# Reordering loads, transposes, a mask and V casts in the opening stage of a fused attention and feed-forward kernel

## The chip, the cores and the metric

The kernel runs on one core of a Trainium2 chip. The metric is the device time of one execution in microseconds (us), lower is better. "Faster" and "slower" are at 2%. Single executions of one kernel here scatter (the kernel before 309.19 to 310.24 us), so every comparison rests on several runs of each kernel on the same chip.

## The reference, cut to what matters

Eight batches of eight heads, 576 positions, head dimension 64, in float32. Attention is causal within a window of 64 positions; its output is then taken through a gated feed-forward layer.

```
scores = scale * q @ k.T;   mask = (rel >= 0) & (rel < 64)
attn   = softmax(where(mask, scores, -1e9))
x      = (attn @ v) as [4608, 512]
h      = x @ w_in                      # w_in  [512, 2048]
g      = h * clip(h + 3, 0, 6) / 6
out    = g @ w_out                     # w_out [2048, 512]
```

## The kernel before

The kernel treats one batch after the other and interleaves two streams on TensorE. While the feed-forward layer of batch b runs ("pieces" of it are released by `run(m, n)` or `go(n)`), the attention of batch b+1 is prepared: Q and K are loaded in float32, cast to bf16 by GpSimd, turned by TensorE (transposes against an identity), copied from PSUM by VectorE or ScalarE, then scores, exponential, mask, product with V. Weights of the feed-forward layer arrive during the same time.

All edits lie in the opening: the first feed-forward stage (batch 0) with the attention of batch 1 beside it, roughly 17 to 56 us of the span. A 576-row sequence is 4 blocks of 128 rows and 64 leftover rows; the "rest" is those leftover rows. `w_out` comes in four parts of 512 KB. Loads issued by GpSimd share one queue, those of SP (the sync engine) another: POOLq and SPq in the profiles.

```
    ld.main(0, 4, 8)                       # Q of heads 4-7 of batch 1, by GpSimd
    ld.main(1, 4, 8)                       # K of heads 4-7
    ...
    bt.cast_qk(st, 0, 0, 4, pcopy)         # pcopy is a GpSimd copy, acopy a ScalarE one
    w_out += [load_w_out(4 * i, 4 * i + 4) for i in (1, 2)]
    bt.cast_rest_runs(rst1, pcopy)
    bt.cast_qk(st, 1, 0, 4, pcopy)
    vst1, end = load_v_end(1)
    after(end, w_out[0], "weights go first")
    rst0, _ = load_rest_runs(0, "rst0")    # rest of Q and K of batch 0, by SP
    rvst0 = load_v_rest_of_first()         # rest of V of batch 0, 128 KB, by SP
    cast_pairs(bt, st, 4, 4)               # casts Q and K of heads 4-7
    w_out.append(load_w_out(12, 16))
    insv = load_v(1, vst1, 0, H, nc.gpsimd)   # V of batch 1, one load for a head
    ...
    bt.main_t(0, 1, h_tr())()
    RR(bt, st_tr(1))                       # rest transposes of batch 1, one bank
    run(m)
    bt.main_t(1, 1, next(st_tr(0)))()      # K transposes of a pair, the other bank
    bt.cast_v_end(vst1, pcopy)
    for h in range(0, H, 2):
        bt.cast_v(vst1, h, h + 2, pcopy)   # two GpSimd casts each
    st2, ins2 = load_for_dma(2, (0,))      # Q of batch 2, by SP
    after(ins2[0], insv[2], "the values go first")
    ...
    def S1_(g, u, bank):
        scores(bt, g, u, bank=bank)()
        if u:
            masked(bt, g)                  # 0.96 us of VectorE, the last one 1.41 us
    ...
    SS1_(3)
    go()
    RR(bt0, st_tr(0))                      # rest of batch 0: transposes, then two copies
    acopy(out=bt0.V[SR:P, KB - 1, :, 0:D], in_=rvst0[SR:P, :, :])
    go(2)
    rest_s(bt0, 1)                         # scores of the rest: reads the copied KT
```

`run` and `go` advance the feed-forward work; `tr`, `st` and `h` are PSUM tiles. The tile framework inserts semaphores from the tiles that instructions touch; the program order on each engine is the order of these statements.

The softmax here doesn't subtract the row's maximum and nothing guards it: scores larger than these inputs give would overflow.

## Time and profile before

| | before |
|---|---|
| median of the first 3 runs | 309.38 us (309.19 to 310.20) |
| median of 6 runs beside the changed kernel | 309.61 us (309.19 to 310.24) |
| span in the profiled execution | 308.9 us, from a run of 310.71 us |
| TensorE busy | 97% |
| next busiest | VectorE and ScalarE, 57% each |
| first feed-forward product of batch 0 starts | 17.63 us |
| from there to the first product of the next token block | 38.86 us |
| from there to the end of TensorE's work | 249.16 us |

The last three rows cut the span at two starts of the same source line. The first of them holds the attention of batch 0, which runs ahead of everything that the change edits. The traces record TensorE's full clock from 4.07 us on in before, and until then a 128x512 matmul takes 634 ns and starts 427 ns after the one before it, afterwards 379 and 216, so the rate starts at half. The second is the stage which the change edits. The third is a stretch in which TensorE is never idle. The profiled run was slower, so a span read from it must not be set against a timed median.

### The profile page before, as it was taken

The page shows a single profiled execution, that of the slowest core. Times are in us where ns is not written, and L with a number is a line of the kernel's source. Part 1 is how long each engine was busy: PE and PEld are TensorE (multiplying, and loading weights), DVE is VectorE, ACT ScalarE, POOL GpSimd, SP SyncE. Part 2 cuts the span into 40 slices and gives each one's busy share as a digit, 9 for nine tenths or more (in the row PEclk, how much of TensorE's full clock was granted, in tenths as well). Part 3 has the DMA queues.
Part 4 walks back from the last instruction along what each step waited for, and adds up shares of the span by engine and source line. Part 5 has one row for each costly group of instructions (what it writes and reads, how often), then busy time and mean ns, then how long its engine had stood idle before and what let it go on. Part 6 is the DMA issues. An engine that isn't in the chain of part 4 may idle for free.

```text
span 308.9 us, 5688 instructions
## 1 busy us (share of the span) xinstructions
PE 300.5 (97%) x2194; PEld 150.2 (49%) x2194; DVE 176.1 (57%) x331; ACT 176.4 (57%) x266; POOL 98.4 (32%) x137
## 2 busy tenths in 40 slices
PE   7899999999999999999999999999999999999995
PEld 3454444644654454445444554455445544444444
DVE  4559545585646882678357834784377537306700
ACT  3857745686737851794179516971588157317711
POOL 5874477634633460426041704071400000000000
PEclk9999999999999999999999999999999999999999
DMA  7999998999999995999999989999910630010011
GB/s 245 201 207 268 259 233 182 245 269 215 189 203 275 206 192 141 246 217 217 171 253 211 216 151 252 208 213 163 245 45 2 134 89 0 34 70 34 0 70 68
DMA packets 141771, 52.80 MB, mean 171 GB/s; under 512 B 128688, under 2 KB 136752, under 8 KB 141744
## 3 DMA queue, kind: packets, MB, share of 16 engines
q1 hardware_dynamic: 135808, 43.73, 71.2%
q0 software_dynamic: 5520, 8.39, 13.0%
q8 instruction: 17, 0.28, 0.4%
q10 hardware_dynamic: 416, 0.33, 0.3%
q14 instruction: 10, 0.08, 0.1%
HBM read 36.70 MB, written 9.44 MB: 149 GB/s over the span
## 4 chain that ended last, share of the span: by engine, by line
PE 85%; DMA 10%; POOL 2%; issue 1%; DVE 1%; SPq 1%; ACT 0%; POOLq 0%
PE o L646 19%; PE acc L646 17%; PE h L580 17%; PE acc L580 6%; PE st L580 6%; PE o L580 6%; DMA qst<-in_q_dram 5%; DMA wout<-in_moe_w_out_dram 4%; PE st L377 4%; PE h L407 2%; PE h L646 2%; PE h L412 1%; DMA vst<-in_v_dram 1%; POOL V L260 1%; POOL win L239 1%
## 5 line engine op out<-in xcount | busy, mean ns | idle before, releaser
L580 PEld LDWEIGHTS <-win 128*128 128x128 bf16 x576 | 54.9, 98 | 63.9 <-DMA win<-in_moe_w_in_dram 0.4
L646 PEld LDWEIGHTS <-gT 128*128 128x128 bf16 x560 | 51.3, 98 | 56.9 <-issue 0.8
L646 PE MATMUL o<-wout,gT 128*128 128x512 bf16 x272 | 66.0, 380 | 0.0
L580 PE MATMUL h<-xT,win 128*128 128x512 bf16 x260 | 62.7, 379 | 0.0
L646 PE MATMUL acc<-wout,gT 128*128 128x512 bf16 x256 | 60.0, 379 | 0.0
L385 ACT ACTIVATE pT<-st 128x768 bf16<-128x768 f32 x64 | 48.5, 808 | 16.6 <-PE st L377 16.5
L588 DVE SCALAR_TENSOR_TENSOR gT<-t,st 128x512 bf16<-128x512 bf16 (+1 forms) x26 | 19.5, 766 | 55.6 <-ACT t L587 55.5
L588 DVE SCALAR_TENSOR_TENSOR gT<-t,h 128x512 bf16<-128x512 bf16 x65 | 43.7, 684 | 11.0 <-ACT t L587 10.9
L587 ACT ACTIVATE t<-h,half 128x512 bf16<-128x512 f32 x65 | 43.9, 692 | 7.7 <-PE h L580 7.7
L395 DVE TENSOR_TENSOR pT<-pT,mask 128x1536 bf16<-128x1536 bf16 x28 | 29.6, 1057 | 23.5 <-ACT pT L385 23.4
L652 ACT COPY osb<-acc 128x512 f32<-128x512 f32 x16 | 9.4, 587 | 42.7 <-PE acc L646 42.7
L260 POOL CAST V<-vst 128x512 bf16<-128x512 f32 (+1 forms) x14 | 17.0, 1221 | 51.7 <-DMA vst<-in_v_dram 51.5
L270 POOL CAST qn<-qst 128x512 bf16<-128x512 f32 x24 | 17.9, 783 | 42.7 <-DMA qst<-in_q_dram 33.1
L580 PE MATMUL st<-xT,win 128*128 128x512 bf16 x120 | 28.9, 379 | 0.0
L652 ACT COPY osb<-o 128x512 f32<-128x512 f32 x17 | 10.0, 588 | 29.4 <-PE o L646 29.4
L580 PE MATMUL acc<-xT,win 128*128 128x512 bf16 x100 | 26.2, 379 | 0.0
L580 PE MATMUL o<-xT,win 128*128 128x512 bf16 x96 | 25.1, 379 | 0.0
L429 DVE TENSOR_TENSOR opg<-h,rec 128x320 bf16<-128x320 f32 x48 | 23.6, 491 | 1.9 <-DVE rec L426 0.3
L587 ACT ACTIVATE t<-st,half 128x512 bf16<-128x512 f32 (+1 forms) x26 | 19.3, 754 | 5.7 <-PE st L580 5.5
L407 PEld LDWEIGHTS <-pT 128*128 128x128 bf16 x256 | 17.4, 97 | 7.6 <-PE h L453 0.5
L587 ACT ACTIVATE t<-acc,half 128x512 bf16<-128x512 f32 x25 | 17.2, 688 | 4.7 <-PE acc L580 4.1
L588 DVE SCALAR_TENSOR_TENSOR gT<-t,acc 128x512 bf16<-128x512 bf16 x25 | 17.1, 684 | 3.5 <-ACT t L587 3.5
(115 smaller groups left out, 296.0 us busy)
## 6 DMA issues: line engine op xcount, KB each, us to landing
out_dram<-osb SPq DMA_DIRECT2D x31, 256.0 KB, 2.5
qst<-in_q_dram SPq DMA_DIRECT2D x28, 256.0 KB, 4.7
vst<-in_v_dram SPq DMA_DIRECT2D x24, 256.0 KB, 5.3
kst<-in_k_dram SPq DMA_DIRECT2D x23, 256.0 KB, 5.6
wout<-in_moe_w_out_dram POOLq DMA_DIRECT2D x4, 512.0 KB, 13.8
vst<-in_v_dram SPq DMA_DIRECT2D x15, 128.0 KB, 3.3
win<-in_moe_w_in_dram POOLq DMA_DIRECT2D x3, 512.0 KB, 8.7
qst<-in_q_dram POOLq DMA_DIRECT2D x2, 512.0 KB, 12.6
```

The costliest lines, as they stand in the source:

```text
L260: copy(out=self.V[:, 0 : KB - 1, h0:h1, 0:D], in_=vst[:, 0 : KB - 1, h0:h1, :])
L270: pcopy(out=n[:, g, 0 : KB - 1, :, :].rearrange("p k h d -> p k (h d)"), in_=s[:, 0 : KB - 1, 2 * g : 2 * g + 2, :].rearrange("p k h d -> ...
L377: nc.tensor.matmul(st[:, h, o0 : o0 + n], lhsT=bt.KT[h * D : (h + 1) * D, g, k0 : k0 + P], rhs=bt.QT[h * D : (h + 1) * D, g, q0 : q0 + n], ...
L385: nc.scalar.activation(out=pT[:, :, 2 * u : 2 * u + 2, 0:QW], in_=st[:, :, 0:w].rearrange("p h (k w) -> p h k w", k=2), func=EXP, scale=scale,
L395: nc.vector.tensor_tensor(out=pT[:, :, :, 0:QW], in0=pT[:, :, :, 0:QW], in1=mask[:].rearrange("p (h k) w -> p h k w", h=2), op=MULT,)
L407: nc.tensor.matmul(ob, lhsT=pT[:, h, qb, 0:P], rhs=V[:, qb, 2 * g + h, :], start=True, stop=(qb == 0),)
L429: nc.vector.tensor_tensor(out=opgs[bt.b, g][:, 0:nb, h, :], in0=ov[:, :, 0:D], in1=rec[:, 0:nb].unsqueeze(2).to_broadcast([P, nb, D]), op= ...
L580: nc.tensor.matmul(hT, lhsT=win16[:, g, fc * P : (fc + 1) * P], rhs=xT[:, g, t0 : t0 + TB], start=(g == 0), stop=(g == NG - 1),)
L587: nc.scalar.activation(out=t1[:], in_=hT, func=RELU, bias=half[:], scale=1.0 / 6.0)
L588: nc.vector.scalar_tensor_tensor(out=out, in0=t1[:], scalar=1.0, in1=hT, op0=MIN, op1=MULT,)
L646: nc.tensor.matmul(accs[ts], lhsT=gT[:, fc, ts * P : (ts + 1) * P], rhs=wout16[:, fc, :], start=(fc == 0), stop=(fc == NFC - 1),)
L652: acopy(out=osb[:], in_=accs[ts])
```

## The change

The intent: bring the second part of `w_out` earlier, so that TensorE does not wait for it; take waits out of the rest transposes; lighten GpSimd by casting V in larger pieces. It has four parts, numbered here as everywhere below: **1** the load of the second `w_out` part goes ahead of K of heads 4-7; **2** the rest transposes use the other bank; **3** the last mask multiply goes behind the drain of the rest transposes of batch 0; **4** V of batch 1 is loaded and cast by blocks of 128 tokens, its last 64 rows by ScalarE.

```diff
     ld.main(0, 4, 8)
+    w_out.append(load_w_out(4, 8))                                  # 1
     ld.main(1, 4, 8)
 ...
-    w_out += [load_w_out(4 * i, 4 * i + 4) for i in (1, 2)]
+    w_out += [load_w_out(4 * i, 4 * i + 4) for i in (2, 3)]         # 1
 ...
-    w_out.append(load_w_out(12, 16))                                # 1
-    insv = load_v(1, vst1, 0, H, nc.gpsimd)
+    insv = load_blocks(vst1, v, 1, (3, 0, 1, 2), eng=nc.gpsimd)     # 4
 ...
-    RR(bt, st_tr(1))
+    RR(bt, st_tr(0))                                                # 2
     run(m)
-    bt.main_t(1, 1, next(st_tr(0)))()
-
-    bt.cast_v_end(vst1, pcopy)
-    for h in range(0, H, 2):
-        bt.cast_v(vst1, h, h + 2, pcopy)
+    bt.main_t(1, 1, next(st_tr(1)))()                               # 2
+
+    for kb in (3, 0, 1, 2):                                         # 4
+        pcopy(out=bt.V[:, kb, :, 0:D], in_=vst1[:, kb, :, :])
 ...
         scores(bt, g, u, bank=bank)()
-        if u:
-            masked(bt, g)
 ...
         S1_(g, 1, 1)
+        if g < NG - 1:                                              # 3
+            masked(bt, g)
 ...
     RR(bt0, st_tr(0))
+    masked(bt, NG - 1)                                              # 3
     acopy(out=bt0.V[SR:P, KB - 1, :, 0:D], in_=rvst0[SR:P, :, :])
     go(2)
     rest_s(bt0, 1)
+    bt.cast_v_end(vst1, acopy)                                      # 4
+    acopy(out=bt.V[0:SR, KB - 1, :, 0:D], in_=vst1[SR:P, KB - 2, :, :])
```

## The prediction

> **What bounds the kernel now.** I read the page first (busy shares, then the slices), then a table of busy time by stretch, then the waits of TensorE inside the one stretch that has any, and last the landing times of the transfers behind those waits.
>
> ```profile
> span 308.9 us, 5688 instructions
> PE 300.5 (97%) x2194; PEld 150.2 (49%) x2194; DVE 176.1 (57%) x331; ACT 176.4 (57%) x266; POOL 98.4 (32%) x137
> ```
>
> TensorE is busy 97% of the span, nothing else over 57%. A change that takes no matmul away can therefore win only TensorE's idle time, 308.9 - 300.5 = 8.4 us in all. Where it lies:
>
> ```profile
> 28.00:32.00 4.00, 3.95 (x27) 1.90 (x25) 3.65 (x7) 2.77 (x5) 1.63 (x3) 1.00 1.18 273
> 32.00:36.00 4.00, 3.46 (x30) 1.92 (x30) 2.36 (x5) 2.73 (x6) 0.51 (x1) 1.00 1.13 275
> 36.00:40.00 4.00, 3.32 (x30) 1.72 (x28) 1.89 (x3) 2.28 (x4) 3.57 (x4) 1.00 1.20 215
> 40.00:44.00 4.00, 4.00 (x33) 2.09 (x32) 1.32 (x3) 1.88 (x3) 4.00 (x7) 1.00 1.21 215
> 48.00:52.00 4.00, 3.37 (x23) 1.35 (x21) 2.51 (x4) 2.35 (x4) 3.69 (x6) 1.00 0.76 172
> 56.00:120.00 64.00, 64.00 (x521) 33.55 (x518) 41.64 (x75) 41.22 (x64) 29.26 (x38) 1.00 1.16 221
> ```
>
> The columns are the stretch, its length, then the busy time of TensorE, weight loads, VectorE, ScalarE and GpSimd, the granted clock, the DMA share and GB/s. From 56 us to 120 us TensorE never idles, and the same table shows 179.96 of 180 us busy from 120 to 300. Only the stretch of 28 to 56 us, which the change edits, has holes: 0.05 + 0.54 + 0.68 + 0.63 + 0.06 (52 to 56 us, 3.94 busy) = 1.96 us. That is the whole prize; the other idle time lies before 20 us and at the end, which the diff does not touch. The waits of TensorE in 27 to 56 us name four:
>
> ```profile
> PE h L646 <- DMA wout<-in_moe_w_out_dram: 0.7, 1, 0.7
> PE st L467 <- ACT osb L652: 0.6, 1, 0.6
> PE st L311 <- DVE gT L588: 0.4, 1, 0.4
> PE st L377 <- ACT KT L345: 0.2, 1, 0.2
> ```
>
> The second label is a coincidence. L467 is the score matmul of the leftover rows of batch 0 and does not read osb; its weight load is listed as waiting 1.1 us for the VectorE copy of KT in L319, which ended at 50.05 us (49.64 + 0.41), and L467 started at 50.10. That copy stood behind a 1.41 us mask multiply.
>
> The first wait is a race of transfers. TensorE, then GpSimd, in order of time:
>
> ```profile
> 38.46 0.39 PE L340 MATMUL st<-ident,qn 128*128 128x128 bf16 x4
> 38.71 0.40 PE L340 MATMUL st<-ident,kn 128*128 128x128 bf16 x4
> 39.78 1.02 PE L646 MATMUL h<-wout,gT 128*128 128x512 bf16 x4 [0.68 <-DMA wout<-in_moe_w_out_dram]
> ```
>
> ```profile
> 35.49 1.04 POOL L292 CAST qn<-qst 128x1024 bf16<-128x1024 f32 x1 [3.99 <-PE st L377]
> 36.96 1.69 POOL L292 CAST kn<-kst 128x1024 bf16<-128x1024 f32 x1 [0.43 <-DMA kst<-in_k_dram]
> ```
>
> The K cast of heads 4-7 ended at 36.96 + 1.69 = 38.65 us, and the K transposes of that pair began at 38.71: K of heads 4-7 has **no slack at all**. Directly after them TensorE waits for the second w_out part. Their issues and landings, one issue each:
>
> ```profile
> kst<-in_k_dram POOLq DMA_DIRECT2D x1, 512.0 KB, 16.4
> wout<-in_moe_w_out_dram POOLq DMA_DIRECT2D x1, 512.0 KB, 13.2
> ```
>
> K was issued at 20.41 us and landed 16.4 us later, at 36.8; w_out part 1 was issued at 26.53 and landed at 39.7. Q of heads 4-7, issued just before K, landed at 19.67 + 15.7 = 35.4. All GpSimd-issued loads from 11 us on land in their order of issue (17.6, 18.8, 21.4, 24.0, 25.4, 28.5, 30.3, 32.6, 35.4, 36.8, 39.7, 43.5, 46.9), and the DMA share is above 1.1 throughout: one saturated queue, first in, first out. After Q, K costs 1.4 us of it and w_out part 1 costs 2.9.
>
> [...]the K cast that met the mask multiply of 36.80 us took 1.69 us, the like-sized Q cast 1.04. [...]No wait of this trace after 20 us is longer than 0.7 us and the granted clock stays at 1.00[...].
>
> **The change part by part.** It adds no matmul and removes none; the instruction orders of both kernels show as many TensorE rows in each.
>
> *1. Second w_out part ahead of K heads 4-7.* It is issued at about 20.4 us between Q and K. In a first-in-first-out queue its landing moves to 35.4 + 2.9 = 38.3 us, and K moves to the end of the same two transfers: 35.4 + 2.9 + 1.4 = 39.7 us.[...] Then the K cast: start 0.15 us after landing (36.96 - 36.81), 1.04 us if no mask multiply meets it, and 0.06 us to the transposes: 39.74 + 0.15 + 1.04 + 0.06 = 41.0 us.[...] They take 0.25 us (38.46 to 38.71 for the Q four), so w_out part 1's first matmuls start at 41.24 instead of 39.78: **+1.46 us**. I take 0.2 us off[...]: **+1.25 us**.
>
> *2. Rest transposes in the other bank.* The new bank was drained by the gate of 30.45 us (done at 31.13), so the 0.42 us wait before 32.38 goes, and with the order of drains most of the 0.17 us before the first scores. TensorE reaches the K transposes about 0.55 us sooner, at 38.15, but waits there for K until 41.0. **Worth 0** while part 1 holds.
>
> *3. Last mask multiply behind the rest drain.* VectorE now does the two L319 copies (0.41 us each) directly after the rest transposes of batch 0, ahead of the 1.41 us mask. Two w_out pieces (2 x 0.86 us) cover them, so the 0.63 us before L467 goes: **-0.63 us**. The mask is wanted by the fourth product with V, about 6 us later.
>
> *4. V by token blocks, tail by ScalarE.* Eight 128 KB loads become four of 256 KB, the same 1 MB; no V load waits for the fourth w_out part any more (GpSimd sat 2.60 us for that at 47.16), and nine GpSimd casts (47.96 to 53.4) become four of 0.61 us. No TensorE wait on V exists today, so nothing is won directly. The risk is that the first product with V now needs all four blocks: last landing about 51.3 as now, plus 0.61 = 51.9, against the product at 52.53 + 0.6 = 53.1. ScalarE gets two copies of about 0.62 us after the exponential of L472 (about 51.8 to 53.05), just ahead of that product, and had 0.37 + 0.28 + 1.24 + 0.41 us idle there to take them. **0, at worst +0.5**.
>
> Sum: +1.25 + 0 - 0.63 + 0 = +0.6 us on 309.38, and 0.1 for part 4: **310.1 us**. Everything later is TensorE-bound, so the shift passes to the end unchanged.
>
> **The rivals.** *A: K comes in time and the change wins.* If loads of this queue could overtake, or the queue drained faster, three waits go: 0.42 + 0.17 + 0.63, and the 0.68 too: up to 1.9 us, 307.5. For it: the author moved this on purpose, and the wait on w_out is visible. Against: 13 landings in order and a cast that ends 0.06 us before its use. *B: the wait at the K transposes, 38.4 to 41.0 = 2.6 us, [...]costs the clock.*[...] *C: V arrives late.* The product of the first pair waits for the last block: +0.5 to +1.5, 310.5 to 311.5. *D: the later Q and V loads of batch 2 shift,* since they are released by the third V load. Hidden: the K casts of batch 2 end at 61.7 and are used at 66.57, V's at 74.5 for 79.24.
>
> **Range and chances.** The ceiling of gain is 1.96 us (0.6%)[...], so 2% either way is nearly out of reach. Two thirds of the weight lie on part 1 as worked out, a fifth on A. Range 308.4 to 311.2. Faster 0.01, within 0.98, slower 0.01.
>
> **What would show it.** Right: a wait of TensorE of about 2.6 us before the second pair's K transposes, released by the GpSimd cast or its K load; no wait on w_out; no wait at L311; L467 without a hole; K landing near 39.7 us; 56 us onward solid. Wrong: K's cast starting before 38.5 us (then A), a clock below 1.00 after 41 us (B), or a wait for V near 53 us (C).

The sum: +1.25 + 0 - 0.63 + 0 = +0.6 us on 309.38 us, and 0.1 us for part 4, make 310.1 us. In it +1.25 is the 1.46 worked out from the landings less 0.2, rounded; the 0.2 is the author's estimate, and no trace gives a reason for it. The clock in the trace of before is 1.00 from 20 to 306 us; it falls at 307.86 us, 2.2 us after TensorE's last matmul (305.65 us).

## The result, and the profile after

The changed kernel took 310.05 us (median of 6 runs, 309.78 to 310.88) against 309.61 us: ratio 1.0014, 95% interval 0.9997 to 1.0031. Ratios here are the mean time of one kernel's runs over that of the other's of the same rounds, so not quite the ratio of the medians. Executions over 1.5% slower than the fastest of the same kernel are left out of the means. The page of the changed kernel, its head:

```profile
span 308.4 us, 5678 instructions
PE 301.6 (98%) x2194; PEld 150.6 (49%) x2194; DVE 176.7 (57%) x331; ACT 177.1 (57%) x268; POOL 91.5 (30%) x128
```

As many TensorE rows as before (2194). GpSimd has 9 instructions fewer and is 6.9 us less busy; ScalarE has the two new copies. The table of busy time by stretch, same columns as in the prediction:

```profile
28.00:32.00 4.00, 4.00 (x26) 1.91 (x23) 3.71 (x7) 2.85 (x5) 1.53 (x2) 1.00 1.17 269
32.00:36.00 4.00, 4.00 (x36) 2.16 (x35) 2.99 (x6) 3.34 (x7) 1.10 (x2) 1.00 1.18 273
36.00:40.00 4.00, 3.39 (x30) 1.76 (x29) 2.07 (x3) 2.03 (x3) 1.82 (x2) 1.00 1.20 213
48.00:52.00 4.00, 3.88 (x37) 1.81 (x36) 1.72 (x4) 2.79 (x5) 1.58 (x3) 1.00 0.53 120
52.00:56.00 4.00, 3.75 (x81) 3.01 (x78) 3.60 (x8) 3.06 (x7) 0.00 (x0) 1.00 1.29 214
56.00:120.00 64.00, 64.00 (x507) 33.19 (x504) 41.39 (x75) 40.95 (x63) 27.99 (x38) 1.00 1.21 223
```

The stretch of 32 to 36 us, which had 0.54 us of idle time at the rest transposes, has none; 48 to 52 us has 0.12 instead of 0.63. One large hole is left, 0.61 us at 36 to 40 us, and 0.25 us in two pieces at 52 to 56 us. From 56 us on TensorE is solid, as before. What TensorE waits for between 27 and 60 us (in all, times, longest):

```profile
PE st L340 <- POOL kn L292: 0.6, 1, 0.6
PE o L453 <- DVE opg L444: 0.2, 1, 0.2
```

All four waits of the kernel before are gone, and the first in their place is the one the prediction named: the K transposes of the second pair wait for the GpSimd cast of K. The same place in order of time, TensorE and then GpSimd:

```profile
38.28 0.39 PE L340 MATMUL st<-ident,qn 128*128 128x128 bf16 x4
39.27 0.40 PE L340 MATMUL st<-ident,kn 128*128 128x128 bf16 x4 [0.61 <-POOL kn L292]
39.51 1.03 PE L646 MATMUL h<-wout,gT 128*128 128x512 bf16 x4
...
49.13 0.29 PE L467 MATMUL st<-QT,KT 64*128 64x64 bf16 x8
```

```profile
34.27 1.04 POOL L292 CAST qn<-qst 128x1024 bf16<-128x1024 f32 x1 [2.20 <-DMA qst<-in_q_dram]
38.18 1.04 POOL L292 CAST kn<-kst 128x1024 bf16<-128x1024 f32 x1 [2.87 <-DMA kst<-in_k_dram]
```

The product with `w_out` at 39.51 us follows the transposes without a wait; its part had landed 3.0 us before, but the transposes stand ahead of it in TensorE's order. L467 at 49.13 us carries no wait any more. The landings, one issue each:

```profile
kst<-in_k_dram POOLq DMA_DIRECT2D x1, 512.0 KB, 16.8
wout<-in_moe_w_out_dram POOLq DMA_DIRECT2D x1, 512.0 KB, 16.2
```

`w_out` part 1 was issued at 20.28 us and landed 16.2 later, at 36.5; K was issued at 21.26 and landed at 38.06. Q of heads 4-7, ahead of both, had landed at 19.51 + 14.6 = 34.1. So K comes 3.9 us after Q; the prediction's queue said 2.9 + 1.4 = 4.3. What differs most from its sum is the landing of Q, 34.1 us instead of 35.4 in the trace of before, although nothing ahead of Q was changed. The queue as a whole did not run earlier: the load just ahead of Q, the first `w_out` part, landed at 32.65 us before and at 32.70 us here.

One thing the prediction did not see. The load of batch 0's leftover V rows, issued by SP at about 36 us in both, from its issue to its landing, before and then after:

```profile
rvst<-in_v_dram SPq DMA_DIRECT2D x1, 128.0 KB, 10.6
```

```profile
rvst<-in_v_dram SPq DMA_DIRECT2D x1, 128.0 KB, 13.1
```

And the ScalarE copy of these rows, before and then after:

```profile
47.96 0.62 ACT L866 CAST V<-rvst 64x512 bf16<-64x512 f32 x1
```

```profile
49.13 0.62 ACT L866 CAST V<-rvst 64x512 bf16<-64x512 f32 x1 [1.47 <-DMA rvst<-in_v_dram]
```

Behind it stand, on ScalarE, the exponential of the rest (`pTr`, at 50.26 us) and the two new tail copies (50.89 and 51.53 us); the last ends at 51.53 + 0.62 = 52.15 us, and TensorE's product with those rows (L418) starts at 52.20 us:

```profile
51.94 0.20 PE L412 MATMUL st<-V,pT 128*128 128x65 bf16 x1
52.20 0.19 PE L418 MATMUL st<-V,pT 128*128 128x65 bf16 x1
```

It starts 0.26 us after the matmul before it, where the distance was 0.02 us in the kernel before. Since matmuls overlap (the one at 51.94 us is listed with 0.20 us), only 0.07 us of this counts as idle; the other 0.18 us of the 0.25 in that stretch lie before L453 at 55.16 us, which waits for VectorE. The 0.12 us of 48 to 52 us lie before L484, which reads `pTr`, further up the same chain.

From the first product of batch 0 to that of the next token block the changed kernel takes 37.56 us where before took 38.86; but it starts at 18.37 us instead of 17.63 (its full clock came at 7.30 us, that of before at 4.07). A repeated look at the same changed kernel gave 38.32 us. One pair of traces thus suggests a gain that the timed runs do not have, and the experiments had to separate the parts by timing.

### The profile page after: what moved, and what is told of

It reads as the page before. It is cut to its first block, busy times and chain, and to the rows that moved or that the text cites. A ratio compares the mean times of both kernels' runs of the same rounds, so it can differ in the third digit from the quotient of the medians.

```text
span 308.4 us, 5678 instructions
## 1 busy us (share of the span) xinstructions
PE 301.6 (98%) x2194; PEld 150.6 (49%) x2194; DVE 176.7 (57%) x331; ACT 177.1 (57%) x268; POOL 91.5 (30%) x128
## 4 chain that ended last, share of the span: by engine, by line
PE 82%; DMA 11%; POOL 2%; SPq 2%; ACT 1%; issue 1%; DVE 0%; POOLq 0%
PE o L646 18%; PE h L580 17%; PE acc L646 17%; PE acc L580 6%; PE st L580 6%; PE o L580 6%; DMA wout<-in_moe_w_out_dram 5%; DMA rvst<-in_v_dram 4%; PE st L377 3%; PE h L407 2%; DMA qst<-in_q_dram 2%; PE h L412 1%; DMA vst<-in_v_dram 1%; POOL win L239 1%; SPq L127 1%
## 5 line engine op out<-in xcount | busy, mean ns | idle before, releaser
L260 POOL CAST V<-vst 128x2048 bf16<-128x2048 f32 (+1 forms) x10 | 13.8, 1393 | 54.0 <-DMA vst<-in_v_dram 54.0
## 6 DMA issues: line engine op xcount, KB each, us to landing
qst<-in_q_dram POOLq DMA_DIRECT2D x2, 512.0 KB, 11.9
```

The costliest lines, as they stand in the source:

```text
L260: copy(out=self.V[:, 0 : KB - 1, h0:h1, 0:D], in_=vst[:, 0 : KB - 1, h0:h1, :])
```

## The experiments

Theory: part 1 only exchanges one wait for another, dearer one, since the load queue is saturated and first in, first out (in the trace of before all 13 landings are in order of issue, and the DMA share is 1.13 to 1.21 from 20 to 44 us); part 2 is worth nothing; part 3 gains about 0.6 us; part 4 is neutral or costs a little. Rivals: the cost comes from part 4 and part 1 gains (rival A of the prediction, with another culprit); a long wait costs the clock (B); V's tail on ScalarE is late (C); the later loads of batch 2 cost (D). Twelve kernels ran, all correct: the first four on one chip, the other eight on a second. Each diff is against the kernel named. For scale: the kernel before had 309.89 us (11 runs, 309.24 to 310.45) on the first chip and 309.91 to 309.94 us (309.54 to 311.28) on the second. Among thirteen intervals one that just excludes 1 proves little by itself. The profiled execution was the slowest of its six in p1_only (311.98 us), p4_only, tail_on_pool (312.13 us) and rvst_first, so a wait read from these traces may be longer than is typical.

| run | parts | median us | ratio to before | 95% interval |
|---|---|---|---|---|
| the first measurement | 1 2 3 4 | 310.05 | 1.0014 | 0.9997 to 1.0031 |
| after_again | 1 2 3 4 | 310.43 | 1.0031 | 1.0003 to 1.0059 |
| p1_only | 1 | 310.46 | 1.0024 | 1.0006 to 1.0043 |
| p1_undone | 2 3 4 | 310.33 | 1.0020 | 0.9991 to 1.0049 |
| p23_only | 2 3 | 309.27 | 0.9974 | 0.9957 to 0.9991 |
| p4_only | 4 | 310.08 | 1.0009 | 0.9987 to 1.0031 |
| tail_on_pool | 1 2 3, 4 without ScalarE | 310.75 | 1.0021 | 1.0006 to 1.0036 |
| two_ahead | 1 doubled, 2 3 4 | 316.28 | 1.0199 | 1.0181 to 1.0218 |
| rvst_first | 2 3 4, leftover V first | 309.92 | 1.0013 | 0.9977 to 1.0049 |
| p23_again | 2 3 | 309.17 | 0.9988 | 0.9963 to 1.0013 |
| p23_late_q | 2 3, batch 2 later | 309.55 | 0.9989 | 0.9966 to 1.0013 |
| undone_early_q | 2 3 4, batch 2 earlier | 309.65 | 0.9992 | 0.9977 to 1.0006 |
| p23_held | 2 3, SP loads later | 317.14 | 1.0189 | 1.0148 to 1.0229 |

### The changed kernel again

No edit. It says how much of a trace and of a ratio repeats.

> The changed kernel once more, to see how much of the traces is chance. Theory Q (the load queue is first in, first out, so K of heads 4-7 lands behind the second w_out part and TensorE waits for its cast): a wait at the second pair's K transposes of 0.5 to 2.6 us in this trace too, w_out part 1 landing before K. Theory S (the timing difference of the two kernels is chance in the first 20 us, where the clock of TensorE starts at half): the time from 28 to 60 us is as in the first trace of the changed kernel, and the start of the first 128x512 product of batch 0 moves by up to 0.8 us. Ratio to the kernel before: 0.999 to 1.003 under both.

310.43 us (309.64 to 312.74), ratio 1.0031. The only wait over 0.2 us in the stage is again that at the K transposes, 0.95 us instead of 0.61. The small cost repeats in sign, and here its interval excludes 1.

### Part 1 alone

Against before:

```diff
     ld.main(0, 4, 8)
+    w_out.append(load_w_out(4, 8))
     ld.main(1, 4, 8)
-    w_out += [load_w_out(4 * i, 4 * i + 4) for i in (1, 2)]
+    w_out += [load_w_out(4 * i, 4 * i + 4) for i in (2, 3)]
-    w_out.append(load_w_out(12, 16))
```

> The kernel before with the second w_out part ahead of K alone. Theory Q: the wait on w_out is gone and a wait at the K transposes takes its place, 0.5 to 1.4 us longer than the 0.68 us removed: ratio 1.002 to 1.005. Rival R (K landed in time after all, the move is free): no K wait, ratio 0.998.

310.46 us (309.77 to 311.98), ratio 1.0024: 0.0024 x 309.89 = 0.74 us slower, with an interval that excludes 1. Its TensorE waits, and its K cast on GpSimd:

```profile
PE st L340 <- POOL kn L292: 2.1, 1, 2.1
PE st L311 <- DVE gT L588: 0.2, 1, 0.2
PE st L467 <- DVE KT L319: 0.2, 1, 0.2
PE st L377 <- ACT KT L345: 0.2, 1, 0.2
```

```profile
39.99 1.16 POOL L292 CAST kn<-kst 128x1024 bf16<-128x1024 f32 x1 [3.16 <-DMA kst<-in_k_dram]
```

Here the cast starts at 39.99 us, where the prediction had 39.74 + 0.15 = 39.9, and the wait is 2.1 us; the prediction's times give 41.0 - 38.71 = 2.3 us for a kernel without part 2. The wait on `w_out` is gone. So part 1 alone has the predicted mechanism, and the timing makes it a small loss.

### Part 1 undone

The changed kernel with the three `w_out` lines of before (the diff of part 1 above, reversed).

> The changed kernel with K ahead of the second w_out part again. Theory Q: TensorE reaches the K transposes at about 38.2 us, K is there at about 38.7, and it waits for w_out part 1 after that: faster than the changed kernel by 0.3 to 1.2 us, so a ratio of 0.996 to 0.999 to the kernel before. Rival R: slower than the changed kernel by 0.7 us (1.002 or more).

310.33 us (309.14 to 312.46), ratio 1.0020 with a wide interval. Against after_again part 1 is worth 1.0031 - 1.0020 = 0.0011, 0.3 us, the same sign as alone, but well inside the intervals. The expectation, 0.996 to 0.999, was missed: without part 1 the kernel should have been faster than before if parts 2, 3 and 4 were harmless together, and no gain shows. Its trace shows a new wait, in ScalarE's view and then TensorE's:

```profile
49.27 0.62 ACT L866 CAST V<-rvst 64x512 bf16<-64x512 f32 x1 [2.15 <-DMA rvst<-in_v_dram]
```

```profile
51.58 0.44 PE L484 MATMUL st<-V,pTr 128*64 128x65 bf16 x8 [0.87 <-DVE pTr L474]
```

ScalarE stands 2.15 us for the leftover V rows of batch 0, the exponential of the rest stands behind that copy, and TensorE waits 0.87 us for its result. The load took 12.5 us from issue to landing.

### Parts 2 and 3 alone

Against before:

```diff
-    RR(bt, st_tr(1))
+    RR(bt, st_tr(0))
-    bt.main_t(1, 1, next(st_tr(0)))()
+    bt.main_t(1, 1, next(st_tr(1)))()
-        if u:
-            masked(bt, g)
+        if g < NG - 1:          # in SS1_
+            masked(bt, g)
     RR(bt0, st_tr(0))
+    masked(bt, NG - 1)
```

> The kernel before with the other bank for the rest transposes and the last mask multiply behind the rest drain, nothing else. If the two waits (0.42 + 0.17 and 0.63 us) are real gains: the 0.63 us before L467 gone, ratio 0.997 to 0.998; the first two are eaten by the wait on w_out. If part 4 costs something in the changed kernel (ScalarE's two copies ahead of the product with V), this one is faster than p1_undone by 0.2 to 0.5 us.

309.27 us (308.48 to 309.85), ratio 0.9974: 0.8 us faster, and the interval excludes 1. All its waits of TensorE in 27 to 60 us:

```profile
PE h L646 <- DMA wout<-in_moe_w_out_dram: 1.2, 1, 1.2
```

The two holes of parts 2 and 3 are gone (0.42 at L311 and 0.63 at L467). But the wait on `w_out` grew from 0.68 to 1.2 us: TensorE came to it 0.87 us sooner (at 39.43 - 1.20 = 38.23 us, before at 39.10), and the part landed only 0.36 us sooner (39.38 us, before 39.74). In this trace what part 2 took away was given back 5 us later, as the prediction had it for the wait at K. That is an account of one trace: p23_again, the same kernel, has only 0.16 us at this wait, and no run times part 2 or part 3 alone.

### Part 4 alone

Against before, the lines marked 4 in the change's diff.

> The kernel before with V by token blocks and its tail cast by ScalarE alone. In the three traces with part 4 the leftover V rows of batch 0 (rvst) landed 12.5 to 13.1 us after issue, in the three without it 10.5 to 11.3, and ScalarE, which copies them in program order, stood 1.4 to 2.2 us. Theory L (part 4 itself delays that load): landing 12.5 us or more here too, ScalarE waiting for it, and a cost of 0.3 to 1.4 us: ratio 1.001 to 1.0045. Rival (part 4 is free, as predicted, and the slow timed runs of the changed kernel are chance): ratio 0.999 to 1.001, no wait.

310.08 us (309.38 to 311.90), ratio 1.0009, +0.3 us, not to be told from nothing. ScalarE's wait for the leftover V rows is 0.80 us (the load took 11.9 us), and TensorE waits for nothing behind it. L467, without part 3, waits 0.2 us only, as in p1_only, where the kernel before had 0.63. The traces show why. The last mask multiply stands ahead of the two L319 copies; in before, where GpSimd cast V beside it (at 47.96 and 48.64 us), it took longer than in p1_only:

```profile
47.97 1.41 DVE L395 TENSOR_TENSOR pT<-pT,mask 128x1536 bf16<-128x1536 bf16 x1 [1.84 <-ACT pT L385]
```

```profile
49.63 0.97 DVE L395 TENSOR_TENSOR pT<-pT,mask 128x1536 bf16<-128x1536 bf16 x1 [1.84 <-ACT pT L385]
```

The other three mask multiplies of before took 0.96 us, and so did this one in p4_only. The 1.41 - 0.96 = 0.45 us more account for 0.63 against 0.18 us of waiting (0.19 in p1_only). GpSimd cast V in p1_only, too, but there the large cast (49.86 us) began after the multiply and was itself the longer one, 1.22 us where its like takes 0.62. The prediction's K cast, too, began after the mask multiply of 36.80 us (36.96 us) and took 1.69 us instead of 1.04. In these pairs the one that began later was the longer; why is not shown. The profiled run was its slowest of six and lost 1.6 us in one wait for `w_in`, which part 4 does not touch, so its span proves nothing.

### V's tail back on GpSimd

The changed kernel with the two tail copies on GpSimd behind the first block's cast:

```diff
         pcopy(out=bt.V[:, kb, :, 0:D], in_=vst1[:, kb, :, :])
+        if kb == KB - 2:
+            bt.cast_v_end(vst1, pcopy)
+            pcopy(out=bt.V[0:SR, KB - 1, :, 0:D], in_=vst1[SR:P, KB - 2, :, :])
-    bt.cast_v_end(vst1, acopy)
-    acopy(out=bt.V[0:SR, KB - 1, :, 0:D], in_=vst1[SR:P, KB - 2, :, :])
```

> The changed kernel with the two V tail copies on GpSimd, between the block casts, instead of ScalarE. If ScalarE's copies are what holds the first product with V (a hole of 0.25 us before L418 at 52.2 in the changed kernel's trace), the hole goes and the time falls by 0.2 to 0.4 us against the changed kernel; if the landing of V blocks or of rvst is what costs, nothing changes (ratio to before 1.001 to 1.003).

310.75 us (310.10 to 312.13), ratio 1.0021. No wait of TensorE is left in 50 to 56 us, so the hole before the product with V fits ScalarE's tail, rival C in small; but ScalarE did not wait for the leftover V rows in this trace either, which ended the tail sooner too. Taking the tail away gained nothing that shows. The wait at the K transposes was 2.1 us in this trace, in the range of p1_only, and with it part 1's cost remains.

### Two parts of w_out ahead of K

The changed kernel with the dose of part 1 doubled:

```diff
     w_out.append(load_w_out(4, 8))
+    w_out.append(load_w_out(8, 12))
     ld.main(1, 4, 8)
-    w_out += [load_w_out(4 * i, 4 * i + 4) for i in (2, 3)]
+    w_out.append(load_w_out(12, 16))
```

> The changed kernel with two w_out parts ahead of K of heads 4-7 (wrong on purpose as a tuning step, right in its result). Theory Q (first in, first out): K lands 2.4 to 2.9 us later than in the changed kernel (about 40.7 us), TensorE waits 3.2 to 3.8 us at the K transposes, and the time rises by 2.4 to 2.9 us (ratio 1.009 to 1.013)[...]. If K could overtake, no more than 0.5 us.

316.28 us (315.42 to 316.62, 4 runs), ratio 1.0199. The waits of TensorE, then the table by stretch:

```profile
PE st L340 <- POOL kn L292: 5.0, 1, 5.0
```

```profile
40.00:44.00 4.00, 0.30 (x4) 0.31 (x5) 0.00 (x0) 0.00 (x0) 1.40 (x2) 0.70 1.12 223
44.00:48.00 4.00, 4.00 (x19) 2.07 (x18) 1.38 (x2) 0.96 (x2) 3.51 (x5) 0.50 0.70 168
```

The same wait at the same place grows to 5.0 us, more than the 3.2 to 3.8 expected: 2.9 more than in p1_only and tail_on_pool, but 4.0 to 4.4 more than in the two traces of the changed kernel. The steadier measure of the dose is the time from Q's landing to K's: 1.5 us in before with no `w_out` part between them, 3.9 to 4.2 us in the four traces with one, 7.8 us here with two. If the queue let K overtake, a second part ahead would have changed nothing. The wait also brought rival B to life: the granted clock falls to half at 41.58 us (the 0.70 is the mean of its stretch) and stays there until 48.41, and 18 weight loads fill 44 to 48 us, where the changed kernel has 30 in the same stretch. The kernel is 6.4 us slower than before, more than the wait itself.

A by-product: GpSimd stands at the K cast until then, so the four V blocks are issued at 43.6 us instead of 39.2 us in the changed kernel, and the leftover V rows of batch 0 land after 9.6 us, not 13.1. That fits V blocks in the queue as what delays them.

### Leftover V rows ahead of the other SP loads

Part 1 undone, with `rvst0 = load_v_rest_of_first()` moved one line up, ahead of `rst0`:

```diff
-    rst0, _ = load_rest_runs(0, "rst0")
     rvst0 = load_v_rest_of_first()
+    rst0, _ = load_rest_runs(0, "rst0")
```

> p1_undone (parts 2, 3 and 4) with the load of the leftover V rows issued ahead of the four loads of leftover Q and K. Theory L: rvst lands before 46 us, the 0.87 us wait at L484 (for pTr, which stands behind the rvst copy on ScalarE) is gone, ratio 0.996 to 0.999. If that wait had another cause it stays and the ratio is 1.001 to 1.003 as in p1_undone.

309.92 us (308.75 to 313.01), ratio 1.0013 with a wide interval. ScalarE's copy at 48.62 us waits for nothing and TensorE's 0.87 us at L484 are gone, so the chain from the late load to that wait is shown. The time did not follow visibly against p1_undone (other chip, 1.0020); the 0.996 to 0.999 expected were missed. The profiled execution was the slowest of its six (313.01 us) and lost 2.4 us after the stage, 251.56 us instead of about 249.2; one of its waits is

```profile
PE h L418 <- POOL V L265: 1.1, 1, 1.1
```

for V of batch 2. That made rival D a candidate: batch 2's loads are released by the third V load, in that kernel the third of four larger blocks.

### Parts 2 and 3 again, and with batch 2 later

The same kernel as p23_only on the second chip, and the same with the release of batch 2's loads delayed from the third to the seventh V load:

```diff
-    after(ins2[0], insv[2], "the values go first")
+    after(ins2[0], insv[6], "the values go first")
```

> p23_only once more, on another chip: whether parts 2 and 3 alone beat both kernels. If the first result was no chance: ratio 0.996 to 0.999, and in the trace no wait at L311 and L467, a wait on w_out of 0.7 to 1.3 us.

309.17 us (308.63 to 311.23), ratio 0.9988; the interval reaches 1.0013, so the gain of p23_only is repeated in sign and, by medians (0.77 us against 0.62), in size, but not in certainty. The wait on `w_out`, expected at 0.7 to 1.3 us, is 0.16 us in this trace.

> p23_only with the first Q load of batch 2 let go by the seventh V load of batch 1 instead of the third: nothing of part 4, only its later start of the batch-2 loads (by about 2 us, to 50.2). Theory D (the batch-2 loads have no slack to spare, so part 4 costs by starting them later): the V casts of batch 2 begin 2 to 3 us later (74 us), a wait of TensorE on V or KT may show between 60 and 95 us, ratio 0.999 to 1.003, so 0.5 to 1.5 us over p23_again. Theory 0 (it is hidden): same time as p23_again within 0.3 us.

309.55 us (308.59 to 311.19), ratio 0.9989, the same as p23_again. The first Q load of batch 2 was issued at 50.43 us instead of 47.63 in p23_again and the V casts of batch 2 began at 73.31 us instead of 70.64. In its trace the later part is 0.7 us longer, but the timed runs do not show that. Rival D as a general cost is not confirmed.

### Part 1 undone, with batch 2 earlier

Against p1_undone, `insv[2]` becomes `insv[1]`, the second of four blocks.

> p1_undone (parts 2, 3, 4) with the first Q load of batch 2 let go by the second V block instead of the third, about 1 us sooner. Theory D: ratio 0.997 to 1.000, so 0.5 to 1.3 us under p1_undone's 1.002, and the V casts of batch 2 begin before 72 us. Theory 0: 1.001 to 1.003 as p1_undone, the loss being the rvst landing alone.

309.65 us (309.17 to 310.21), ratio 0.9992. It is parts 2, 3 and 4 with an earlier release, and is level with p23_again (0.9988): there part 4 costs 0.0004, 0.1 us. ScalarE still waits 1.59 us for the leftover rows, but TensorE's wait at L484 is 0.2 us only. Against p1_undone (1.0020) this speaks for D, but the two ran on different chips and their intervals overlap.

### The SP loads held back

p23_only with the SP loads of the leftovers released by the second `w_out` part, to leave the queue to that part:

```diff
-    after(end, w_out[0], "weights go first")
+    after(end, w_out[1], "weights go first")
```

> A try at a version better than p23_only: its SP-queue loads of leftover rows are let go by the second w_out part instead of the first, so that fewer transfers run beside K and w_out part 1. Gain expected: w_out part 1 lands 0.5 to 1 us sooner, ratio 0.994 to 0.997. Rival: the held loads then crowd w_out part 2, which has no slack either, or land too late for the casts at 45 to 48 us: ratio 0.998 or more.

A miss: 317.14 us (313.39 to 318.18; one of six runs slow and left out of the ratio), ratio 1.0189. The `w_out` wait went, but the rest of Q and K of batch 0 now came far too late. TensorE's longest wait in 27 to 60 us, and the table by stretch:

```profile
PE st L311 <- DVE rn L303: 5.8, 1, 5.8
```

```profile
48.00:52.00 4.00, 0.00 (x0) 0.00 (x0) 0.01 (x1) 0.00 (x0) 1.26 (x3) 0.69 1.20 178
52.00:56.00 4.00, 3.38 (x11) 1.47 (x12) 2.18 (x4) 0.62 (x1) 3.62 (x7) 0.50 1.03 199
```

It is the second kernel with a wait above 4 us and the second in which the clock halves (from 49.52 us on), at another line and with another cause. No wait up to 2.14 us (tail_on_pool) lowered it.

## Why the prediction was right or wrong

The time was right: 310.1 us predicted, 310.05 measured. Part of that is luck of the base: the prediction added 0.7 us to 309.38 us, and measured were 0.44 us over 309.61, with an interval that reaches from -0.1 to +1.0 us. The steps fared differently.

**What bounds the kernel: right.** All that moved was in 17 to 56 us; the part behind it stayed at about 249.2 us. Even the best version gains 0.1 to 0.3%, within the prize of 1.96 us.

**Part 1, +1.25 us: right in mechanism, too large in size.** Disappearance of the `w_out` wait, place and releaser of the new wait are as told, and two_ahead confirms the queue by its dose. In all fourteen traces GpSimd's loads of the opening landed in order of issue. (The DMA share was not above 1.1 throughout, as the prediction has it: 1.09 from 12 to 20 us, 0.96 from 44 to 48.) The size: the wait at the K transposes was 0.61, 0.95, 2.1 and 2.14 us in the four traces with one part ahead, 1.45 on average, against 2.6; the two long ones are from executions that were the slowest of their six. And the wait on `w_out` that it replaces is no constant 0.68 us: in the eight traces with K first and the SP loads not held it was 0.68, 1.20, 1.26, 0.16 and four times none, on average 0.41. The difference, 1.0 us, is an estimate from scattered traces; the timed cost is 0.74 us alone and 0.3 us on top of the other parts.

The failed term is "35.4" in the landing sum. In the changed kernel K's cast began at 38.18 us and not at 39.9: 1.3 us of that is Q's landing, 0.4 the two transfers behind it (3.9 us, not 4.3). TensorE, too, came to the transposes at 39.27 - 0.61 = 38.66 us, later than in either of the prediction's figures, which do not agree: 38.4 us gives its 2.6, the 38.15 of its part 2 would give 2.85. The 0.2 us that it took off has no number behind it. Q's landing is no constant; its cast started between 34.2 and 36.6 us in the traces here, and every landing after it shifts along. From the landing of the first `w_out` part to Q's it took 1.40 to 1.48 us in the six traces with V by blocks, its tail on ScalarE and the SP loads in place, and 1.97 to 2.99 us in the other eight, p1_only among them. So part 1 may cost less beside part 4 than alone. GpSimd's V loads are issued only after Q has landed, so the cause is open.

**Part 2, worth 0: its waits go** (nothing at L311 in the changed kernel), and in the changed kernel and in p23_only TensorE waits at the next stop. In p23_again it hardly does (0.16 us), and part 2 was never timed alone, so its worth without part 1 stays open.

**Part 3, -0.63 us: right in mechanism, sized from one trace.** The hole at L467 is gone in the changed kernel, and parts 2 and 3 together measure -0.8 and -0.4 us by ratio. But the prediction took the mask multiply at 1.41 us, where the other three of the same trace took 0.96; p1_only and p4_only, which keep the old order and have the short multiply, wait 0.2 us there. So part 3 is worth 0.2 us or 0.6, as the multiply falls out.

**Part 4, "0, at worst +0.5": the step that is least sound.** The path that was worked out, the last V block and its cast against the product with V, is fine: the last GpSimd cast ends at 49.10 + 1.33 = 50.43 us. What was missed is another load that runs beside V's: from 34 to 39.5 us in the changed kernel the packets of one queue (q0) took 103.5% of the 16 DMA engines' time and those of another (q1) 14.1%. The leftover V rows of batch 0 take 11.9 to 13.1 us in the six traces with V by blocks in which neither they nor the blocks were moved, and 10.5 to 11.7 us in the five with V by heads and the SP loads in place. GpSimd issues the megabyte of V within 3.5 us from 39.16 us on in the changed kernel, where before it took 5.2 us for seven eighths of it and held the last back until 47.16 us; together with two_ahead this points to V's bytes being ahead of those rows, though no run doubles or halves them. ScalarE, which had no wait there in the kernel before (and up to 0.6 us in other kernels with V by heads), stands 0.8 to 2.15 us for them in five of the six, and its slack, which the prediction counted as free for the tail copies, is spent. The cost in time is +0.3 us alone, 0.0020 + 0.0026 = 0.0046 or 1.4 us by difference, and 0.1 us with batch 2 released earlier. Its sign is likely; its size stays open.

Since the sizes of part 1 and part 4 erred in opposite directions, the sum, too, was right partly by luck: 0.74 for part 1, -0.4 to -0.8 for parts 2 and 3 and +0.3 for part 4 make +0.2 to +0.6 us, against 0.44 measured in the first comparison.

**The rivals.** A is refuted by the order of the landings and by the wait that two_ahead lengthens, and part 1's own timing speaks against it, though the sign that the prediction gave for A did appear: K's cast started at 38.18 us, before 38.5. That sign was badly chosen, for it tested an absolute time that shifts from run to run and not the wait. B did not happen in the changed kernel (clock 1.00, wait 0.61 us) and happened in both kernels with waits of 5.0 and 5.8 us. There the clock fell 2.84 and 2.70 us after TensorE's last matmul, so the predicted wait of 2.6 us would have ended 0.1 to 0.2 us short of the fall. C happened in small, about 0.25 us, without visible effect on the time. D is neither shown nor ruled out for kernels with part 4; for parts 2 and 3 a 2.8 us later start cost nothing that shows.

**The best version** by medians is parts 2 and 3 without 1 and 4: 309.27 and 309.17 us on two chips, where before has 309.89 and 309.94, and the changed kernel 310.43 on the first of them.

## What to carry to other kernels

When loads share one saturated queue and land in their order of issue, as in all fourteen traces here, pulling one ahead can take its wait from one consumer and give it to the next: here 0.68 us at `w_out` went and 0.61 us at K came. First look how much slack the overtaken load has, which was 0.06 us here. Before crediting a removed wait, find the next one on the same engine: in p23_only what was gained at L311 was paid again at the `w_out` wait. Before sizing a gain by one wait, look at whether the instruction behind it had its usual length: the 1.41 us multiply was 0.45 us longer than its like. When the prize is below 1% of the time, split a compound change and time the parts with their intervals: here parts 2 and 3 gained together, part 1 probably lost, and a single pair of traces showed a gain of the stage that the timed runs do not have.

## What else the traces show

- Landings scatter, and a reshaped load on one queue can go with a later landing on another: Q of heads 4-7 landed at 35.4 us in one trace and 34.1 us in another with the same work ahead of it (the load before it at 32.65 and 32.70 us), and the 128 KB SP load took 10.6 us in the kernel with V loaded by heads and 13.1 us in that with V loaded by blocks.
- The granted clock falls in a long wait: at 41.58 us in two_ahead, 2.84 us after TensorE's last matmul had ended (43.70 - 4.96 = 38.74 us), and at 49.52 us in p23_held, 2.70 us after (52.62 - 5.80 = 46.82 us). Both low stretches lasted 6.83 us. Waits of up to 2.14 us left the granted clock at 1.00; the runs do not probe between 2.14 and 5.0 us.
- Matmul records are missing from some traces. In p23_again the stretch from 120 to 300 us has 1153 matmul rows against 1173 weight loads and shows 1.2 us of idle time, where the changed kernel's trace has 1173 and 1172 and shows 0.02; the time from the first product of the next token block to the end is the same, 249.26 and 249.28 us. All eight traces of the second chip have 2158 matmul rows against 2194 weight loads; why is not shown. The idle time that this trace shows is not real:

```profile
120.00:300.00 180.00, 178.78 (x1153) 86.44 (x1173) 100.89 (x176) 100.11 (x151) 34.03 (x42) 1.00 0.71 140
```
